# Powers on VectorE for chunk pairs, one contraction a chunk and a fixed instruction sequence in a gated mix of a diagonal state-space convolution and a gated linear unit

## The chip, the cores and the metric

The kernel runs on one core of a Trainium2 chip. The metric is the time of one execution on the device, in microseconds. The engines that matter are TensorE (PE in the profile, with its weight loads as PEld), VectorE (DVE), ScalarE (ACT), GpSimd (POOL), and SP, which issues nearly all DMAs.

## The reference, cut to what matters

All arrays are fp32: L = 2048 positions, D = 448 channels, N = 256 states, F = 1792 hidden units.

```python
dt = exp(log_dt)                                  # per channel
A  = -exp(log_A_real) + 1j * A_imag               # (D, N)
C  = (C_real + 1j * C_imag) * dt[:, None]
P  = exp((A * dt[:, None])[:, :, None] * arange(L))
K  = 2 * einsum("dn,dnl->dl", C, P).real          # the filter, (D, L)
y  = irfft(rfft(u.T, 2 * L) * rfft(K, 2 * L))[:, :L].T
a  = y + u * D_skip
b  = (sigmoid(u @ w_gate) * (u @ w_up)) @ w_down
g  = sigmoid((u * gate_w).sum(-1))
out = g * a + (1 - g) * b
```

## The kernel before, in words

Five kinds of work share the engines. (1) The gate `g`. (2) `params`: per half of the channels, amplitudes, phases and decay powers go through DRAM (`phd`, `bsd`). (3) `kgen`, the filter stage: 28 chunks of 16 channels make the filter `K`. (4) `Chain`: the convolution by an FFT written as matmuls, for two halves, with transposes through DRAM (`shf`) or, for one chain, on VectorE. (5) the gated unit: `glu_up`, `glu_mm` and `glu_down`, fp32 products as three matmuls of split operands (`wh`, `wl`, `xs`, `hh`, `hl`, `vh`, `vl`).

A position is l = 32 b + r. The filter of one channel is contracted over the 256 states from two factors, one for each part of the position; each factor is an amplitude (powers of the decay) times a sine or a cosine. In one chunk (`kgen`), for each of the two halves of the states (`half_chunk`, the states on the partitions):

- `turns` makes the angles with a matmul (`tp`, L1128), rounds them to whole turns on ScalarE (L1138, L1139), takes the whole turns off with a second matmul (L1141), and ScalarE makes `Abs` and `Sin` (L1143, L1144); L1158 makes the cosine. Cosines lie in `ec`, sines in `fr`.
- `powers` makes a table `tb` of decay powers, by GpSimd, one table for each chunk: (128, 32, 28), that is 16 channels of each of two halves of the states, and 28 powers of each, next to each other. Its instructions are L1105 to L1118.
- `outer` (L1165) multiplies two sets of those powers into the 96 amplitudes of each channel, in `es`: one VectorE product of 1024 elements (8 x 8 for 16 channels) and one of 512 (4 x 8).
- L1179 and L1181 (512 elements each) and L1183 and L1185 (1024 each) multiply amplitudes with cosines and sines, in `ec` and `es`.
- `g` contracts the half chunk (L1191): two sets of 16 products on quarters of the array's columns, into `kp`. After the second half ScalarE copies `kp` into `ke` (L1215), with a step of 56 elements in what it writes.

After 14 chunks a half of the filter goes to DRAM (`kd`) and its chain starts. The gated unit's matmuls fill TensorE between all this.

The order of the instructions on each engine is made before the kernel runs. `Plan.op` records each operation with what it reads and writes; `Plan.order` plays the program through a model of the engines (`Clock`) and emits, at each step, the ready operation with the lowest rank, where `RANK` gives ranks to groups of operations by engine, tile and priority. The engines then run these sequences in order, each waiting on semaphores.

Of the kernel before, what the change touches and what calls it, by code (L numbers as in the profile page):

```python
# [20 lines left out]
HD = 224  # L21
# [3 lines left out]
LADV = 0  # L25
CHANGE = 0.0


RANK = {
    ('Act', 'aci', 10): (671, -492),  # L30
    ('Act', 'aci', 19): (-256.5, 733.5),
    ('Act', 'acr', 10): (800, 106.5, -694.5),
    ('Act', 'acr', 19): (339, 607, -637),
    ('Act', 'ai', 10): 814,
    ('Act', 'ai', 19): -138,
    ('Act', 'bsx0', 10): (209.5, 93),
    ('Act', 'bsx0', 19): (192.5, 209),
    ('Act', 'ci', 10): (895.5, -362.5, 445.5),
    ('Act', 'ci', 19): (-615.5, 239, -615.5),
    ('Act', 'cr', 10): 118.5,  # L40
    ('Act', 'cr', 19): 618,
    ('Act', 'dots', 1): -520.5,
    ('Act', 'dots', 2): 579.5,
    ('Act', 'dots', 16): (-700, 879.5),
# [14 lines left out]
    ('Act', 'junk', 10): (143, 528),  # L59
    ('Act', 'junk', 19): (-337, -331.5, -344),  # L60
# [28 lines left out]
    ('DVE', 'aci', 10): 103,  # L89
    ('DVE', 'aci', 19): -245.5,  # L90
    ('DVE', 'acr', 10): 424.5,
    ('DVE', 'acr', 19): 900,
    ('DVE', 'ai', 10): -291.5,
    ('DVE', 'ai', 19): 529.5,
    ('DVE', 'bsx0', 10): (-548, 25),
    ('DVE', 'bsx0', 19): (-490.5, 740.5),
    ('DVE', 'ci', 10): 214.5,
    ('DVE', 'ci', 19): -661.5,
    ('DVE', 'cr', 10): (-364.5, 16.5),
    ('DVE', 'cr', 19): (93, -700),  # L100
    ('DVE', 'dt2', 10): -119,
    ('DVE', 'dtp', 10): 809.5,
    ('DVE', 'dtv', 10): 562.5,
    ('DVE', 'ec', 20): (492, 737, -509, -522.5, -148, -508.5, -540.5, -401.5),
    ('DVE', 'es', 20): (-560.5, -700, -613.5, -700, -577.5, -249, -611.5, -666.5),
    ('DVE', 'f', 10): (-484.5, -600.5),
    ('DVE', 'fx', 41): (-696.5, -696.5, -667, -700, 254, 114.5, -225.5, 268),
    ('DVE', 'gs', 1): 257.5,
    ('DVE', 'gs', 2): -362,
    ('DVE', 'gs', 16): (804, 891.5),  # L110
    ('DVE', 'gt', 1): (503.5, 457, 457, 457),
    ('DVE', 'gt', 2): (-418.5, -378, -416, -419),
    ('DVE', 'gt', 16): (-250.5, 93.5, -505.5, -522, -583.5, -600, -260, 548),
    ('DVE', 'half_pi', 0): 423.5,
# [20 lines left out]
    ('DVE', 'ones', 10): -432,  # L135
# [6 lines left out]
    ('DVE', 'skip', 20): 361,  # L142
# [5 lines left out]
    ('DVE', 'uax', 40): (733.5, -443, -259, 207, 252.5, -43, 547, -200.5),  # L148
# [1294 lines left out]
```

## Time and profile before

| | us |
|---|---|
| median of 3 runs (lowest to highest) | 742.1 (741.53 to 743.33) |
| the profiled execution's own time | 740.59 |
| its span, first to last instruction | 738.8 |
| granted clock of TensorE, mean | 0.979 |
| busy: PE, DVE, ACT, POOL | 688.4, 637.9, 523.7, 232.7 |

A row that groups instructions has the line, the engine and the operation, what it writes and reads, its shape and its count, then the time busy, the mean of one in ns, and the engine's idle time just before them with what ended it. A row of one line gives shortest, median and longest duration in ns and the first and the last start. A row of the chain of waits or of the timeline has its start and its length in us; on the chain a length ends where the next piece takes over. A row of stretches has the stretch, its length, each engine's busy time with its number of instructions, the granted clock, the DMA engines' share and GB/s.

### The profile page before, as it was taken

What the parts mean: (1) busy time and instruction counts of PE and PEld (TensorE: products, weight loads), DVE (VectorE), ACT (ScalarE), POOL (GpSimd) and SP (SyncE); (2) the same over time, 40 slices, a digit from 0 to 9 for tenths busy, and PEclk for the clock granted to TensorE, in tenths of its full rate; (3) what the DMA queues carried; (4) which work ended last, traced back from release to release, by engine and by line L of the source; (5) the groups of instructions that cost most, each with busy time, mean ns of one, the idle gap of its engine ahead of it and who ended that gap; (6) DMA issues with size and microseconds to landing.
All of it is one profiled execution on the core that took longest, in us unless ns stands there. A gap on an engine that the chain in (4) does not pass through costs nothing.

```text
span 738.8 us, 16536 instructions
## 1 busy us (share of the span) xinstructions
PE 688.4 (93%) x6628; PEld 498.6 (67%) x6628; DVE 637.9 (86%) x847; ACT 523.7 (71%) x962; POOL 232.7 (32%) x282
## 2 busy tenths in 40 slices
PE   4999899999999999978998899999999899999996
PEld 3788777677757776745666677777778566445863
DVE  6999998999999979999898779999995259775976
ACT  5578749999899779998998789999882342233110
POOL 0043446563455435434543324654400000000000
PEclk9999999999999999988999899999999999999998
DMA  9658337925949945469797913239516963787975
GB/s 291 200 122 217 108 79 203 239 91 171 202 121 223 219 107 160 171 175 204 183 232 180 220 45 125 86 133 175 119 40 131 271 226 100 249 304 207 168 191 142
DMA packets 98660, 126.12 MB, mean 171 GB/s; under 512 B 31224, under 2 KB 81080, under 8 KB 97560
## 3 DMA queue, kind: packets, MB, share of 16 engines
q1 hardware_dynamic: 98328, 124.61, 65.0%
q8 instruction: 52, 0.85, 0.5%
q0 software_dynamic: 256, 0.46, 0.3%
q14 instruction: 24, 0.20, 0.1%
HBM read 81.46 MB, written 43.58 MB: 169 GB/s over the span
## 4 chain that ended last, share of the span: by engine, by line
PE 42%; DVE 19%; ACT 16%; DMA 14%; issue 5%; SPq 3%; POOL 2%; ACTq 0%; DVEq 0%
PE kp_egp L1191 4%; PE gu_gps L1296 4%; PE dn_gps L1313 4%; PE gu_gps L1297 4%; PE gu_gps L1298 4%; PE dn_gps L1314 3%; PE dn_gps L1315 3%; DMA fx_fu<-shf 3%; SPq L615 3%; DVE es_eg L1165 2%; PE tp_egp L1128 2%; PE tp_egp L1141 2%; ACT nn_eg L1139 2%; DMA us<-fx_fu 2%; PE fps_fups L716 2%
## 5 line engine op out<-in xcount | busy, mean ns | idle before, releaser
L1296 PE MATMUL gu_gps<-xs_glu,wh_glu 128*128 128x512 f32 x336 | 138.1, 411 | 16.5 <-ACT wh_glu L1270 10.1
L1298 PE MATMUL gu_gps<-xs_glu,wl_glu 128*128 128x512 f32 x336 | 133.2, 397 | 0.4 <-DVE wl_glu L1272 0.4
L1297 PE MATMUL gu_gps<-xs_glu,wh_glu 128*128 128x512 f32 x336 | 133.3, 397 | 0.0
L1165 DVE TENSOR_TENSOR es_eg<-tb_eg 128x1024 f32<-128x1024 f32 x112 | 107.4, 988 | 7.0 <-POOL tb_eg L1115 3.7
L1313 PE MATMUL dn_gps<-vh_glu,hh_glu 128*128 128x448 f32 x224 | 87.9, 393 | 2.8 <-DVE ob_glu L1329 2.6
L1296 PEld LDWEIGHTS gu_gps<-xs_glu,wh_glu 128*128 128x128 f32 x336 | 64.1, 191 | 39.2 <-ACT wh_glu L1270 10.1
L1115 POOL TENSOR_TENSOR tb_eg<-tb_eg 128x96 f32<-128x96 f32 (+2 forms) x84 | 82.2, 982 | 6.2
L1314 PE MATMUL dn_gps<-vh_glu,hl_glu 128*128 128x448 f32 x224 | 82.6, 369 | 0.6 <-issue 0.4
L1315 PE MATMUL dn_gps<-vl_glu,hh_glu 128*128 128x448 f32 x224 | 82.3, 368 | 0.0
L1139 ACT ACTIVATE nn_eg<-fr_eg 128x512 fp32r<-128x512 f32 x112 | 75.0, 669 | 10.3 <-PE tp_egp L1141 10.1
L1329 DVE SCALAR_TENSOR_TENSOR ob_glu<-dn_gps,og,ob_glu 128x448 f32<-128x448 f32 x72 | 48.7, 677 | 30.2 <-PE dn_gps L1315 30.0
L1298 PEld LDWEIGHTS gu_gps<-xs_glu,wl_glu 128*128 128x128 f32 x336 | 64.0, 191 | 15.6 <-DVE wl_glu L1272 1.1
L1297 PEld LDWEIGHTS gu_gps<-xs_glu,wh_glu 128*128 128x128 f32 x336 | 64.2, 191 | 11.4
L1105 POOL MEMSET tb_eg<- 128x96 f32 x28 | 7.8, 283 | 201.1 <-DVE es_eg L1165 200.9
L1144 ACT ACTIVATE fr_eg<-tp_egp 128x512 f32<-128x512 f32 x112 | 69.9, 629 | 0.3 <-PE tp_egp L1141 0.3
L1185 DVE TENSOR_TENSOR es_eg<-fr_eg,es_eg 128x1024 f32<-128x1024 f32 x56 | 69.8, 1246 | 0.1
L1143 ACT ACTIVATE ec_eg<-tp_egp 128x512 f32<-128x512 f32 x112 | 69.4, 625 | 0.3 <-PE tp_egp L1141 0.2
L1183 DVE TENSOR_TENSOR ec_eg<-ec_eg,es_eg 128x1024 f32<-128x1024 f32 x56 | 69.5, 1241 | 0.1
L1138 ACT ACTIVATE fr_eg<-tp_egp 128x512 f32<-128x512 f32 x112 | 64.0, 636 | 7.2 <-DVE es_eg L1185 5.1
L1158 ACT ACTIVATE ec_eg<-ec_eg,half_pi 128x1024 f32<-128x1024 f32 x56 | 67.1, 1197 | 0.1
L1118 POOL TENSOR_TENSOR tb_eg<-tb_eg,bs_eg 128x32 f32<-128x32 f32 x84 | 62.0, 741 | 6.2
L1284 ACT ACTIVATE sg_glu<-gu_gps 128x512 f32<-128x512 f32 x56 | 34.0, 608 | 37.5 <-PE gu_gps L1301 35.3
(154 smaller groups left out, 1423.0 us busy)
## 6 DMA issues: line engine op xcount, KB each, us to landing
shf<-fx_fu SPq DMA_DIRECT2D x16, 896.0 KB, 4.1
fx_fu<-shf SPq DMA_DIRECT2D x16, 896.0 KB, 15.9
us<-fx_fu SPq DMA_DIRECT2D x16, 896.0 KB, 6.7
xr_glu<-in_w_dram SPq DMA_DIRECT2D x52, 256.0 KB, 3.0
ua_fk<-us SPq DMA_DIRECT2D x16, 448.0 KB, 6.0
uax_fk<-us SPq DMA_DIRECT2D x16, 448.0 KB, 4.5
vr_glu<-in_w_dram SPq DMA_DIRECT2D x28, 224.0 KB, 5.1
gt_pre<-in_u_dram SPq DMA_DIRECT2D x8, 448.0 KB, 4.9
```

Of the source, the lines that this page charges most:

```text
L1115: pool(96 * m, lambda n=n, m=m: G.tensor_mul(g3(n + 1, m), g3(1, m), g3(n, 1).to_broadcast([128, 32, 3, m])))
L1139: op("Act", c_act(512), lambda: S.activation(nn.real, fi(), AF.Copy, scale=-1.0, bias=MAGIC), [(fr, i)], [nn], prio)
L1144: op("Act", c_act(512, True), lambda: S.activation(fr[:, ds], tv(), AF.Sin, scale=TWO_PI), [tp], [(fr, i)], prio, table="sin")
L1165: V.tensor_mul(o.rearrange("p d (i k) -> p d i k", k=ny), x.unsqueeze(3).to_broadcast([128, 16, nx, ny]), y.unsqueeze(2).to_broadcast([128 ...
L1183: op("DVE", c_dve(1024), lambda: V.tensor_mul(ec[:, :, 32:96], ec[:, :, 32:96], es[:, :, 32:96]), [(es, 1), (es, 2)], [(ec, "p")], prio)
L1185: op("DVE", c_dve(1024), lambda: V.tensor_mul(es[:, :, 32:96], fr.real, es[:, :, 32:96]), [fr], [(es, 1), (es, 2)], prio)
L1296: T.matmul(p.real, wh[:, k, cs], x[:, k], start=(k == 0), stop=False)
L1297: T.matmul(p.real, wh[:, k, cs], x[:, 4 + k], start=False, stop=False)
L1298: T.matmul(p.real, wl[:, k, cs], x[:, k], start=False, stop=False)
L1313: T.matmul(p[:, :D], hh[:, ts], vh.real, start=(i == 0), stop=False)
L1314: T.matmul(p[:, :D], hl[:, ts], vh.real, start=False, stop=False)
L1315: T.matmul(p[:, :D], hh[:, ts], vl.real, start=False, stop=(i == len(fs) - 1))
```

## The change

- `powers` runs on VectorE, once for a pair of chunks. Its table is (128, 29, 64): 29 powers, and for each the 64 columns (two halves of the states by 32 channels) next to each other. There is one table instead of two; the decay powers' place in `bsd` is reordered for it. `outer` reads the table with channels and powers swapped in the access pattern.
- Cosines and sines lie in one tile `cs` (128, 2, 16, 96), three of them; the two products of 1024 elements are one of 2048, with the amplitudes read twice. `es` has one buffer.
- `contract` does both half chunks in one block, after the second.
- The four steps of a gated unit's matmuls wait for the halves of the activations and weights that they read, not for all.
- `vr` shares the raw tiles `xr` (4 now; 5 and one `vr` before); `sg` has 2 buffers for 3, `bs` 1 for 2; the phases are loaded for each chunk.
- The identity and the positions are loaded by SP and rounded by ScalarE; before, GpSimd's queue loaded them.
- `PLACE` gives every operation its place in its engine's sequence, in the stead of ranks; the model only merges the sequences, with issue times for each DMA.

```diff
-WB, ECB, FRB, TPB, KPB, GUB, FPS, SGB, XRB = 3, 2, 2, 2, 1, 2, 2, 3, 5
+WB, CSB, PHB, BSB, TPB, KPB, GUB, FPS, SGB, XRB = 3, 3, 2, 1, 2, 1, 2, 2, 2, 4
...
-        for key, x in RANK.items():
-            x = x if isinstance(x, tuple) else (x,)
-            for j, o in enumerate(kinds[key]):
-                o["prio"] = x[j * len(x) // len(kinds[key])]
+        for key, places in PLACE.items():
+            for o, place in zip(kinds[key], places, strict=True):
+                o["place"] = place
...
-    def powers(c, bs, prio):
-        tb = eg.tile("tb", TBB, (128, 32, 28))
+    def powers(bs, prio):
+        tb = state.get("tb")
+        if tb is None:
+            tb = state["tb"] = eg.tile("tb", 1, (128, 29, 64))
+            op("DVE", c_fast(192), lambda: V.memset(tb[:, 0:24].rearrange("p (g e) x -> p g e x", e=8)[:, :, 0], 1.0),
+               [], [(tb, 0)], prio)
         def g3(lo, n):
-            return tb[:, :, 0:24].rearrange("p d (g e) -> p d g e", e=8)[:, :, :, lo:lo + n]
+            return tb[:, 0:24].rearrange("p (g e) x -> p g e x", e=8)[:, :, lo:lo + n]
...
+        mul(256, lambda: V.tensor_copy(tb[:, 1:26:8], bs[:, 0:4]), c_fast)
         for n in (1, 2, 4):
             m = min(n, 3)
-            pool(96 * m, lambda n=n, m=m: G.tensor_mul(g3(n + 1, m), g3(1, m), g3(n, 1).to_broadcast([128, 32, 3, m])))
+            mul(192 * m, lambda n=n, m=m: V.tensor_mul(g3(n + 1, m), g3(1, m), g3(n, 1).to_broadcast([128, 3, m, 64])))
+        for e in range(25, 28):
+            mul(64, lambda e=e: V.tensor_mul(tb[:, e + 1], tb[:, e], bs[:, 4]))
...
         def r(k):
-            tt = tb[:, q0:q0 + 16]
+            tt = tb[:, :, q0:q0 + 16].rearrange("p e d -> p d e")
             if k == 0:
                 outer(es[:, :, 0:64], tt[:, :, 8:16], tt[:, :, 0:8])
...
-        op("DVE", c_dve(1024), lambda: V.tensor_mul(ec[:, :, 32:96], ec[:, :, 32:96], es[:, :, 32:96]),
-           [(es, 1), (es, 2)], [(ec, "p")], prio)
-        op("DVE", c_dve(1024), lambda: V.tensor_mul(es[:, :, 32:96], fr.real, es[:, :, 32:96]),
-           [fr], [(es, 1), (es, 2)], prio)
+        op("DVE", c_dve(2048), lambda: V.tensor_mul(
+            cs[:, :, :, 32:96], cs[:, :, :, 32:96], es[:, :, 32:96].unsqueeze(1).to_broadcast([128, 2, 16, 64])),
+           [(es, 1), (es, 2)], cos + sin, prio)
+        return cs
+
+    def contract(parts, kp, prio):
         def g():
-            for e in (ec, es):
-                for q in range(4):
-                    for j in range(4):
-                        T.matmul(kp[32 * j:32 * j + 32, q], e[:, 4 * j + q, 64:96], e[:, 4 * j + q, 0:64], ...)
-        op("PE", c_mm4(64, 32, QUARTERS), g, [ec, es], [kp], prio)
+            for cs in parts:
+                for z in range(2):
+                    for q in range(4):
+                        for j in range(4):
+                            T.matmul(kp[32 * j:32 * j + 32, q], cs[:, z, 4 * j + q, 64:96], cs[:, z, 4 * j + q, 0:64], ...)
+        op("PE", c_mm4(64, 64, QUARTERS), g, parts, [kp], prio)
...
-            op("PE", c_mm(512, 3 if k < 3 else 2), lambda k=k: g(k), [x, wh, wl], [p], pe)
+            z = 2 * (k // 2)
+            op("PE", c_mm(512, 3 if k < 3 else 2), lambda k=k: g(k), [(x, (0, z)), (x, (1, z)), (wh, z), (wl, z)], [p], pe)
```

More of the change, by code (lines that the diff above doesn't have):

```diff
@@ new lines @@
+PLACE = {
+    ('Act', 'aci', 10): (19, 46,),
+    ('Act', 'aci', 19): (73, 100,),
+    ('Act', 'acr', 10): (15, 44, 57,),
+    ('Act', 'acr', 19): (78, 97, 109,),
[26 rows of a table added]
+    ('Act', 'dots', 1): (39,),
+    ('Act', 'dots', 2): (53,),
+    ('Act', 'dots', 16): (71, 87,),
[18 rows of a table added]
+    ('Act', 'idn', 10): (20,),
+    ('Act', 'junk', 10): (42, 77,),
+    ('Act', 'junk', 19): (89, 96, 122,),
[12 rows of a table added]
+    ('Act', 'pos_sb', 10): (32, 98,),
[24 rows of a table added]
+    ('DVE', 'aci', 10): (56,),
+    ('DVE', 'aci', 19): (127,),
+    ('DVE', 'acr', 10): (91,),
+    ('DVE', 'acr', 19): (167,),
[17 rows of a table added]
+    ('DVE', 'dtp', 10): (46,),
+    ('DVE', 'dtv', 10): (33,),
[14 rows of a table added]
+    ('DVE', 'half_pi', 0): (2,),
[22 rows of a table added]
+    ('DVE', 'ones', 10): (0,),
[7 rows of a table added]
+    ('DVE', 'skip', 20): (30,),
[11 rows of a table added]
+    ('DVE', 'uax', 40): (734, 738, 744, 745, 755, 754, 763, 764, 768, 767, 774, 773, 777, 778, 785, 784, 811, 812,
[131 rows of a table added]
@@ L243 @@
 HB = 3
-PEM = (1, 1)
 GLO = 0
@@ L367, in run @@
         if o["size"]:
-            self.free[e] = t + (self.ISSUE if e == "SP" else self.CAST)
+            self.free[e] = t + (o["issue"] if e == "SP" else self.CAST)
             self.wire = max(self.wire, self.free[e] + 1000.0) + o["cost"]
@@ L474, in order @@
         clock = Clock(engines)
-        cand = {e: [o for o in ops if o["eng"] == e and need[o["i"]] == 0] for e in engines}
+        queue = {e: sorted((o for o in ops if o["eng"] == e), key=lambda o: -o["place"]) for e in engines}
         users, done, left, end, slots = {}, {}, {}, {}, {}
@@ L485, in start_of @@
         def start_of(o):
+            if need[o["i"]]:
+                return None
             t, n = ready[o["i"]], {}
@@ L502, in order @@
             for e in engines:
-                lo, ok = None, []
-                for o in cand[e]:
-                    t = start_of(o)
-                    if t is not None:
-                        ok.append((t, o))
-                        lo = t if lo is None else min(lo, t)
-                if lo is None:
-                    continue
-                te = clock.when(e, lo)
-                if best is None or te < best[0]:
-                    best = (te, e, ok)
+                t = start_of(queue[e][-1]) if queue[e] else None
+                if t is not None:
+                    te = clock.when(e, t)
+                    if best is None or te < best[0]:
+                        best = (te, e)
             if best is None:
                 raise RuntimeError("no instruction can start")
-            te, e, ok = best
-            def rank(o):
-                change = e == "PE" and clock.mode is not None and o["cost"][0][0] != clock.mode
-                return o["prio"] + (CHANGE if change else 0.0), o["i"]
-            o = min((o for t, o in ok if t <= te), key=rank)
-            cand[e].remove(o)
+            te, e = best
+            o = queue[e].pop()
             fin = clock.run(o, te)
@@ L543, in order @@
                 need[d] -= 1
-                if need[d] == 0:
-                    cand[p["eng"]].append(p)
             seq.append((te, len(seq), o))
@@ L698, in stage1 @@
                     dma(lambda ls=ls, z=z: x[64 * z:64 * z + 64, ls], lambda ls=ls: ap()[:, ls], 64 * 4 * HD * 4, src,
-                        [(x, (z, r)) for r in range(4 * q, 4 * q + 4)], prio, HALF)
+                        [(x, (z, r)) for r in range(4 * q, 4 * q + 4)], prio, HALF, 700.0)
             for q in range(4):
@@ L877, in gated_mix @@
     P = 112
-    steps, POW = (64.0, 1.0, 512.0, 8.0), (2, 0, 3, 1)
+    steps, POW = (64.0, 1.0, 512.0, 8.0), (2, 0, 4, 1)
     class Params:
@@ L1113, in powers @@
         for n in (1, 2, 4):
             m = min(n, 3)
-            pool(96 * m, lambda n=n, m=m: G.tensor_mul(g3(n + 1, m), g3(1, m), g3(n, 1).to_broadcast([128, 32, 3, m])))
-        pool(32, lambda: G.tensor_scalar(t(24), b(4), 1.0, 0.0, op0=ALU.mult, op1=ALU.add), c_pool1)
-        for e in range(24, 27):
-            pool(32, lambda e=e: G.tensor_mul(t(e + 1), t(e), b(3)))
+            mul(192 * m, lambda n=n, m=m: V.tensor_mul(g3(n + 1, m), g3(1, m), g3(n, 1).to_broadcast([128, 3, m, 64])))
@@ L1151, in half_chunk @@
+        op("Act", c_act(512, True), lambda: S.activation(cs[:, 1, ds, 32:96], block(tp), AF.Sin, scale=TWO_PI),
+           [tp], [(cs, ("s", i))], prio, table="sin")
+    def half_chunk(c, nh, ph, tb, prio):
+        cs = eg.tile("cs", CSB, (128, 2, 16, 96))
+        es = eg.tile("es", 1, (128, 16, 96))
         for i in range(2):
             tp = egp.tile("tp", TPB, (128, 512))
-            turns(c, nh, i, ph, fr, tp, ec, on_pe, prio)
-        if not on_pe:
-            op("Act", c_act(1024), lambda: S.activation(ec[:, :, 32:96], fr.real, AF.Abs), [fr], [ec], prio)
-            op("Act", c_act(1024), lambda: S.activation(fr.real, fr.real, AF.Sin, scale=-TWO_PI), [], [fr], prio,
-               table="sin")
+            turns(c, nh, i, ph, cs, tp, prio)
+        cos, sin = [(cs, ("c", i)) for i in range(2)], [(cs, ("s", i)) for i in range(2)]
@@ L1198, in kgen @@
         if c % 2 == 0:
-            ph = state["ph"] = eg.tile("ph", 2, (96, 2, N))
-            for i in range(2):
-                dma(lambda i=i: ph[:, i], lambda i=i: phd[:, 16 * (c + i):16 * (c + i) + 16], 96 * 1024,
-                    [(phd, (k, c // 14)) for k in range(6)], [(ph, i)], prio, 115.0)
-            bs = state["bs"] = eg.tile("bs", 2, (128, 5, 64))
+            bs = state["bs"] = eg.tile("bs", BSB, (128, 5, 64))
             dma(lambda: bs.real, lambda: bsd[:, c // 2].rearrange("p (a d) -> p a d", a=5), 128 * 1280,
                 [(bsd, (i, c // 14)) for i in range(5)], [bs], prio)
-        ph, tb = state["ph"], powers(c, state["bs"], prio)
+            powers(bs, prio)
+        tb, ph = state["tb"], eg.tile("ph", PHB, (96, N))
+        dma(lambda: ph.real, lambda: phd[:, 16 * c:16 * c + 16], 96 * 1024,
+            [(phd, (k, c // 14)) for k in range(6)], [ph], prio, 115.0, 700.0)
         if cc == 0:
@@ L1210, in kgen @@
         kp = egp.tile("kp", KPB, (128, 4, 64))
-        for nh in range(2):
-            half_chunk(c, nh, ph, tb, kp, prio)
+        contract([half_chunk(c, nh, ph, tb, prio) for nh in range(2)], kp, prio)
         def ev():
@@ L1263, in glu_w @@
             glu_split(wr, lambda wr=wr: wr.real, wh, wl, lambda t, k=k: t[:, k:k + 2], k, 512, prio, 7 * H + f // 2)
-        vr = glu.tile("vr", 1, (128, D))
-        dma(lambda: vr.real, lambda: w2[128 * f:128 * f + 128], 128 * D * 4, [], [vr], prio)
-        glu_split(vr, lambda: vr.real, vh, vl, lambda t: t.real, 0, D, prio, 7 * H + f // 2)
+        vr = raw_tile(H == 0 and f < 2)
+        vw = lambda: vr.v("p a b -> p (a b)")[:, :D]
+        dma(vw, lambda: w2[128 * f:128 * f + 128], 128 * D * 4, [], [vr], prio)
+        glu_split(vr, vw, vh, vl, lambda t: t.real, 0, D, prio, 7 * H + f // 2)
         ws[H, f] = (wh, wl, vh, vl)
@@ L1376, in gated_mix @@
     params(1, sizes, P_PRO1)
+    for i in range(2):
+        rounded(pos, post, 96, 512, 512 * i)
     kgen_consts(P_E)
```

152 lines of the change are left out of this document (40 added, 112 removed), and 438 rows, old and new, of tables (PLACE, RANK).

## The prediction

> **What bounds the kernel now.** I read the page's head first, then busy time by stage, then the groups by shape, and last the chain at both ends of the filter stage.
>
> ```profile
> span 738.8 us, 16536 instructions
> ## 1 busy us (share of the span) xinstructions
> PE 688.4 (93%) x6628; PEld 498.6 (67%) x6628; DVE 637.9 (86%) x847; ACT 523.7 (71%) x962; POOL 232.7 (32%) x282
> ```
>
> PE leads on the whole span, but the change acts in one stage. The filter stage runs from the first outer product at 123.7 us to the last VectorE multiply, started at 553.4 us:
>
> ```profile
> L1165 DVE TENSOR_TENSOR es_eg<-tb_eg x112: 673/1207/1855, 123.7 to 548.6; 128x1024 f32<-128x1024 f32 x56, 128x512 f32<-128x512 f32 x56
> ...
> L1185 DVE TENSOR_TENSOR es_eg<-fr_eg,es_eg x56: 1206/1214/1893, 132.5 to 553.4; 128x1024 f32<-128x1024 f32 x56
> ...
> L1179 DVE TENSOR_TENSOR ec_eg<-ec_eg,es_eg x56: 673/692/1398, 128.7 to 549.9; 128x512 f32<-128x512 f32 x56
> ```
>
> Busy time in the stretches before, in and after it:
>
> ```profile
> core 0: us, PE busy (x) PEld busy (x) DVE busy (x) ACT busy (x) POOL busy (x), PEclk, DMA share, GB/s
> 0.00:127.00 127.00, 110.75 (x487) 90.39 (x488) 114.22 (x213) 87.65 (x156) 44.14 (x48) 1.00 0.64 174
> 127.00:555.00 428.00, 405.46 (x5050) 295.82 (x5048) 402.87 (x480) 388.68 (x718) 188.60 (x234) 0.97 0.64 157
> 555.00:739.00 184.00, 172.19 (x1094) 112.40 (x1093) 120.86 (x157) 47.34 (x90) 0.00 (x0) 0.98 0.72 200
> ```
>
> In the filter stage PE, DVE and ACT are busy 405, 403 and 389 of 428 us: three engines within a few per cent of each other. VectorE has 25 us of room there. More VectorE work than that lengthens the stage; the 63 us that it is idle after 555 us are out of reach, since the tail needs the finished filter. So the prediction is a VectorE sum over this stage, plus what happens at its two ends.
>
> **Part 1, powers leave GpSimd.** VectorE's groups in the stage, by shape, and the longest wait of all:
>
> ```profile
> L1165 DVE TENSOR_TENSOR es_eg<-tb_eg 128x1024 f32<-128x1024 f32 x56 | 69.8, 1246 | 6.3 <-POOL tb_eg L1115 3.7 <-PE kp_egp L1191 1.3 <-POOL tb_eg L1108 0.5
> L1185 DVE TENSOR_TENSOR es_eg<-fr_eg,es_eg 128x1024 f32<-128x1024 f32 x56 | 69.8, 1246 | 0.1
> L1183 DVE TENSOR_TENSOR ec_eg<-ec_eg,es_eg 128x1024 f32<-128x1024 f32 x56 | 69.5, 1241 | 0.1
> L1179 DVE TENSOR_TENSOR ec_eg<-ec_eg,es_eg 128x512 f32<-128x512 f32 x56 | 45.0, 804 | 10.2 <-ACT ec_eg L1158 9.8
> L1181 DVE SCALAR_TENSOR_TENSOR es_eg<-fr_eg,es_eg 128x512 f32<-128x512 f32 x56 | 42.2, 754 | 0.5
> L1165 DVE TENSOR_TENSOR es_eg<-tb_eg 128x512 f32<-128x512 f32 x56 | 40.9, 730 | 0.6 <-POOL tb_eg L1118 0.6
> L1288 DVE TENSOR_TENSOR hl_glu<-sg_glu,hh_glu 128x512 fp32r<-128x512 f32 x56 | 39.5, 713 | 7.1 <-ACT hh_glu L1287 7.0
> L1272 DVE TENSOR_TENSOR wl_glu<-xr_glu,wh_glu 128x512 fp32r<-128x512 f32 x52 | 37.9, 749 | 0.0
> ...
> POOL tb_eg L1105 <- DVE es_eg L1165: 200.9, 26, 12.4
> ```
>
> GpSimd waited 201 us for a free table, so its powers were ahead of need except at the start; taking them away ends waits of only some 5 us (3.7, 0.6, 0.5). What VectorE gains is duration. The quickest 1024- and 512-wide operations took 1206 and 673 ns; the means lie above by 40, 40 and 35 ns on the wide ones and by 131, 81, 57, 40 and 76 ns on the narrow ones. Times 56 (52 for the last) that is 28 us; some of L1272 and L1288 lies outside the stage, so I credit 26, on the reading that GpSimd's arithmetic causes all of it. The bound from below is 0.
>
> What comes back as VectorE work, per chunk pair: a copy of 256 elements, products of 192, 384 and 576, three of 64. Durations overlap the next instruction, so steps in the chain price them better:
>
> ```profile
> 110.81 3.70 DMA bs_eg<-bsd
> ...
> 114.58 2.79 POOL tb_eg L1108 x2
> 117.37 4.12 POOL tb_eg L1115 x6
> 121.50 1.22 POOL tb_eg L1116 x2
> 122.71 2.93 POOL tb_eg L1118 x5
> ...
> 138.16 1.13 DVE ec_eg L1183
> ...
> 141.63 0.60 DVE ec_eg L1179
> 142.23 0.54 DVE vl_glu L1272
> 142.77 0.60 DVE es_eg L1181
> 143.37 1.74 DVE es_eg L1165 x2
> ```
>
> 1024 in 1.13 and 512 in 0.60 us give 1.035 ns an element and 0.07 us an instruction. The products: 0.27 + 0.47 + 0.67 + 3 x 0.14 = 1.83; the copy 0.2 to 0.33, taken 0.2. So 2.03 us a pair, 28 us for 14: the relief and the new work cancel.
>
> **Part 2, the layout of the table.** This edit is not in the name of the change. Before, the table is (32 channels, 28 powers), and the eight powers that the outer product's second operand runs through lie next to each other; its first operand holds one element for eight results. These reads go at full speed (1.74 for 1024 + 512, as 1.13 + 0.61). After, it is (29 powers, 64 channels): the second operand steps 64 elements, 256 bytes, at every result. The trace shows no such VectorE product. Its nearest rows are operations that step far at every element:
>
> ```profile
> L730 DVE STREAM_TRANSPOSE fx_fk<-fx_fk 128x896 f32<-128x896 f32 x16 | 31.1, 1966 | 1.7 <-ACT fx_fk L719 1.7
> L1215 ACT ACTIVATE ke_eg<-kp_egp 128x256 f32<-128x256 f32 x28 | 19.5, 696 | 4.3 <-PE kp_egp L1191 4.3
> L719 ACT ACTIVATE fx_fk<-fps_fkps 128x448 f32<-128x448 f32 x16 | 7.8, 543 | 16.8 <-PE fps_fkps L716 16.8
> ...
> 604.91 3.69 DVE L730 STREAM_TRANSPOSE fx_fk<-fx_fk 128x896 f32<-128x896 f32 x2 [1.66 <-ACT fx_fk L719]
> ```
>
> The transpose reads and writes with a step of 224 elements: two in 3.69 us, about 1.80 each, (1.80 - 0.07) / 896 = 1.93 ns an element, 0.89 above the plain rate. ScalarE's copy of 256 elements with a written step of 56 took 696 ns where 448 elements in long runs took 543: at least 0.60 ns an element dearer, on one stepping side. So the price for one stepping operand lies between 0 (if transposing itself is what costs) and 0.89 (if the read alone makes it); half of the transpose's excess is 0.45. I take 0.65, between that half and the whole, near ScalarE's one-sided 0.60. A half chunk has 1024 + 512 such elements: 1.0 us, times 56 = 56 us; bounds 0 and 77.
>
> The Trainium skill's page "Vector Engine (DVE) Microarchitecture Reference", section "Measured stream behaviour on trn2", says that a port keeps its full rate only over runs of at least two adjacent 4-byte words: 1.73 ns a column with one source jumping at every element against 1.054 contiguous, and 1.98 with all operands jumping. By that the edit costs an estimated 58 us; the transpose's 1.93 agrees with its 1.98, and no run here shows the one-source case. The same table has 2.50 for a step of 24 words, which would make it an estimated 125 us.
>
> **Part 3, sine and cosine in one tile.** Two 1024-wide products (1.13 each) become one of 2048: 2048 x 1.035 ns + 0.07 = 2.19, so -0.07 x 56 = -4 us.
>
> **Part 4, one contraction a chunk.** On PE, around one contraction of before:
>
> ```profile
> 200.02 0.39 PE L1297 MATMUL gu_gps<-xs_glu,wh_glu 128*128 128x512 f32 x1
> 200.25 0.39 PE L1298 MATMUL gu_gps<-xs_glu,wl_glu 128*128 128x512 f32 x1
> 200.57 0.65 PE L1191 MATMUL kp_egp<-ec_eg 128*32 128x64 f32 x32
> 201.04 0.63 PE L1191 MATMUL kp_egp<-es_eg 128*32 128x64 f32 x32
> 201.60 0.50 PE L1300 MATMUL gu_gps<-xs_glu,wh_glu 128*128 128x512 f32 x1
> 201.94 0.40 PE L1301 MATMUL gu_gps<-xs_glu,wl_glu 128*128 128x512 f32 x1
> ```
>
> Starts are 0.23 us apart in a run, 0.32 into the contraction and 0.34 after it: 0.2 us a change of form. 28 fewer save at least 5.6 us of PE. I count nothing: PE is no longer what ends the stage. If Part 2 costs nothing, this is what keeps PE (405 busy) clear of VectorE. The contraction now waits for both halves; behind it on PE stand the gated unit's matmuls, and ScalarE's half after next waits for the tile. With three tiles it can run one half ahead, which is 1.74 + 0.60 + 0.60 + 2.19 = 5.1 us of VectorE work and covers two blocks of 1.03 (200.57 to 201.60); nothing counted.
>
> **Part 5, gated unit by quarters; loads; one raw tile fewer.** Units may start on half the weights; PE's gain is hidden as in Part 4. The copies of identity and positions leave GpSimd's queue for three more issues on SP and three short ScalarE copies, in the first 127 us, where ScalarE is busy 88: hidden. Each chunk's phase load waits on SP for the chunk two before, and the raw weight loads behind it with it; with four shared raw tiles for six, 0, up to the 25 us of slack.
>
> **Part 6, the fixed sequence.** Counting it off: 32, 31, 32 and 35 of VectorE's sg, hl, wl and ob steps lie in the stage, against 29, 27, 28 and 32 in the trace: 14 more at 0.60, +8 us. The first contraction stands behind 113 steps on gu, of 135 before. The stage's start: from the landed amplitudes (110.81 + 3.70 = 114.5) GpSimd's tables let the first outer product begin at 123.7, 9.2 us later; VectorE needs 2.0: -7. Of the 8 us moved out from ahead of it some 3 come off as well, and of the 22 gu steps (2.75 matmuls of 0.23 us each, 14 us of PE) I add 2. Start 123.7 -> 112. In the tail PE, 172 of 184 us busy, has nearly the same steps: 184 kept.
>
> **Sum.** VectorE in the stage: 403 - 26 + 28 + 56 - 4 + 8 = 465 us; with 13 us of idle (half of now, as it is alone the bound) 478. 112 + 478 + 184 = 774 us of span. The profiled execution took 740.59 us for its 738.8, so +1.8: **775 us**, against that 740.59 (the median of the runs is 742.1). About 0.3%, 2.2 us, is what can be told from no change.
>
> **Rivals.** (a) *Steps are free*, and the 1.93 ns are the transpose's own. VectorE 409, idle 15: 112 + 424 + 184 = 720, **722 us**, faster. For it: a read repeated eight times already costs nothing. Against: ScalarE's row, which transposes nothing. (b) *The read alone costs the whole 0.89 or more*: 77 us, **797 us** and up; its lower edge is where the read takes more than the write. (c) *The order stalls though steps are free*: phase and weight loads behind one another on SP leave VectorE idle for twice today's 25 us instead of 15: 722 + 35 = **757 us**; for it only ScalarE's waits of 9.8 us ahead of L1179 stand, which show how little is spare.
>
> **How the numbers follow.** Forecast 0.62 (its own range 757 to 797), (a) 0.22, (b) 0.10, (c) 0.04, and 0.02 that gains and price cancel. Slower 0.76, same 0.02, faster 0.22. The range of 8 in 10 takes in most of (a) and the foot of (b): 716 to 805.
>
> **What would show it.** Right: the 1024-wide outer product near 1.9 us (1.25 now), the 512-wide near 1.05, the other 512-wide ones at 0.68, VectorE over 96% busy in the stage, PE below 90%, first outer product near 112 us. Wrong: outer products at 1.21 us; then (a) or (c), told apart by the stage's length. A tail far from 184 us would break the sum's last term.

## The result, and the profile after

| | before | after |
|---|---|---|
| median of the runs (lowest to highest) | 742.25 (741.53 to 743.33) | 779.48 (777.94 to 781.22) |
| after : before, 95% interval | | 1.0501 (1.0471 to 1.0531) |
| the profiled execution, its span | 740.59, 738.8 | 778.36, 776.6 |
| stage starts, first outer product | 123.7 | 118.0 |
| stage, first outer product to the end of the last VectorE product | 430.9 | 480.2 |
| from there to the end | 184.2 | 178.4 |

All in us. One of the four executions in experiment 2 (817.74 us) was in a slower state and is left out there. The change made the kernel 5% slower. The filter stage grew by 49.3 us; its start and the tail gave back 11.5.

The head of the page and its chain of work that ended last, after, and then the same line of the chain before:

```profile
span 776.6 us, 16302 instructions
## 1 busy us (share of the span) xinstructions
PE 695.5 (90%) x6628; PEld 502.4 (65%) x6628; DVE 705.8 (91%) x890; ACT 532.1 (69%) x965; POOL 29.3 (4%) x28
...
## 4 chain that ended last, share of the span: by engine, by line
DVE 49%; PE 33%; issue 10%; ACT 6%; DMA 2%; SPq 0%; DVEq 0%; ACTq 0%
```

```profile
PE 42%; DVE 19%; ACT 16%; DMA 14%; issue 5%; SPq 3%; POOL 2%; ACTq 0%; DVEq 0%
```

VectorE now has more busy time than PE, and half of the chain, where it had a fifth. Busy time by stretch, after, cut at the stage's own ends (columns as before):

```profile
core 0: us, PE busy (x) PEld busy (x) DVE busy (x) ACT busy (x) POOL busy (x), PEclk, DMA share, GB/s
0.00:118.00 118.00, 101.49 (x430) 81.28 (x431) 104.84 (x211) 83.35 (x149) 29.33 (x28) 0.99 0.63 164
118.00:598.00 480.00, 421.97 (x5098) 307.58 (x5097) 477.60 (x521) 401.01 (x726) 0.00 (x0) 0.96 0.57 144
598.00:776.00 178.00, 172.00 (x1101) 113.50 (x1101) 123.32 (x160) 47.77 (x91) 0.00 (x0) 1.00 0.78 212
```

In the stage VectorE is busy 477.6 of 480 us, 99.5%, and PE 422, 88%. VectorE alone sets its length. What it does there, its groups by shape, after:

```profile
L1242 DVE TENSOR_TENSOR cs_eg<-cs_eg,es_eg 128x2048 f32<-128x2048 f32 x56 | 128.2, 2289 | 0.6
L1223 DVE TENSOR_TENSOR es_eg<-tb_eg 128x1024 f32<-128x1024 f32 x56 | 117.7, 2101 | 0.4
L1223 DVE TENSOR_TENSOR es_eg<-tb_eg 128x512 f32<-128x512 f32 x56 | 61.7, 1102 | 0.0
...
L1239 DVE SCALAR_TENSOR_TENSOR cs_eg<-cs_eg,es_eg 128x512 f32<-128x512 f32 x56 | 38.4, 687 | 0.0
L1237 DVE TENSOR_TENSOR cs_eg<-cs_eg,es_eg 128x512 f32<-128x512 f32 x56 | 38.4, 686 | 0.1
```

The outer products went from 1246 and 730 ns to 2101 and 1102. The two 512-wide products with cosines and sines went the other way, from 804 and 754 to 686 and 687, with GpSimd quiet. One group of PE says who waits now, the gated unit's `dn` matmuls, after and then before:

```profile
L1376 PE MATMUL dn_gps<-vh_glu,hh_glu 128*128 128x448 f32 x224 | 89.8, 401 | 26.0 <-DVE ob_glu L1392 20.7
```

```profile
L1313 PE MATMUL dn_gps<-vh_glu,hh_glu 128*128 128x448 f32 x224 | 87.9, 393 | 2.8 <-DVE ob_glu L1329 2.6
```

PE stood 20.7 us for VectorE's step that reads that PSUM tile. Before, the whole idle time of this group was 2.8 us. And the start of the stage, in the chain of waits, after (start, length):

```profile
106.28 0.20 DVE tb_eg L1182
...
109.13 0.14 DVE tb_eg L1185
...
111.51 0.47 DVE tb_eg L1185
111.97 0.54 DVE th_pro L975
112.51 0.67 DVE tb_eg L1185
113.18 0.54 DVE th_pro L978
113.72 0.59 DVE ob_glu L1392
...
116.85 0.13 DVE tb_eg L1187
...
118.12 2.09 DVE es_eg L1223 x2
```

The powers are made from 106 us on, between steps of the parameters (`pro`) and of the gated unit on the same engine. The chain passes through VectorE's own queue and no longer through a landed load: the load of the decay powers (`bs`) is issued at 96.1 us now, at 110.8 before.

### The profile page after: what moved, and what is told of

The parts are those of the page before. It is cut to its first block, busy times and chain, and to the rows that moved or that the text cites. A ratio compares the mean times of both kernels' runs of the same rounds, so it can differ in the third digit from the quotient of the medians.

```text
span 776.6 us, 16302 instructions
## 1 busy us (share of the span) xinstructions
PE 695.5 (90%) x6628; PEld 502.4 (65%) x6628; DVE 705.8 (91%) x890; ACT 532.1 (69%) x965; POOL 29.3 (4%) x28
## 4 chain that ended last, share of the span: by engine, by line
DVE 49%; PE 33%; issue 10%; ACT 6%; DMA 2%; SPq 0%; DVEq 0%; ACTq 0%
DVE es_eg L1223 13%; DVE cs_eg L1242 11%; PE gu_gps L1358 4%; DVE cs_eg L1239 4%; DVE cs_eg L1237 4%; PE gu_gps L1359 4%; PE gu_gps L1360 4%; PE dn_gps L1376 3%; PE dn_gps L1377 3%; DVE ob_glu L1392 3%; PE dn_gps L1378 3%; DVE tb_eg L1185 3%; DVE wl_glu L1334 2%; DVE sg_glu L1347 2%; DVE hl_glu L1350 2%
## 5 line engine op out<-in xcount | busy, mean ns | idle before, releaser
L1223 DVE TENSOR_TENSOR es_eg<-tb_eg 128x1024 f32<-128x1024 f32 x112 | 175.7, 1602 | 0.4
L1358 PE MATMUL gu_gps<-xs_glu,wh_glu 128*128 128x512 f32 x336 | 139.6, 416 | 20.7 <-DVE sg_glu L1347 9.7
L1359 PE MATMUL gu_gps<-xs_glu,wh_glu 128*128 128x512 f32 x336 | 135.4, 403 | 0.0
L1242 DVE TENSOR_TENSOR cs_eg<-cs_eg,es_eg 128x2048 f32<-128x2048 f32 x56 | 128.2, 2289 | 0.6
L1376 PE MATMUL dn_gps<-vh_glu,hh_glu 128*128 128x448 f32 x224 | 89.8, 401 | 26.0 <-DVE ob_glu L1392 20.7
L1198 ACT ACTIVATE cs_eg<-tp_egp 128x512 f32<-128x512 f32 x112 | 67.2, 604 | 20.0 <-PE tp_egp L1194 18.8
L1376 PEld LDWEIGHTS dn_gps<-vh_glu,hh_glu 128*128 128x128 f32 x224 | 43.0, 192 | 54.8 <-DVE ob_glu L1392 32.9
L1200 ACT ACTIVATE nn_eg<-cs_eg 128x512 fp32r<-128x512 f32 x112 | 71.3, 637 | 9.6 <-PE tp_egp L1203 8.4
L1205 ACT ACTIVATE cs_eg<-tp_egp 128x512 f32<-128x512 f32 x112 | 66.0, 602 | 12.8 <-PE tp_egp L1203 12.5
L1206 ACT ACTIVATE cs_eg<-tp_egp 128x512 f32<-128x512 f32 x112 | 67.3, 604 | 8.1 <-PE tp_egp L1203 7.9
L1359 PEld LDWEIGHTS gu_gps<-xs_glu,wh_glu 128*128 128x128 f32 x336 | 65.3, 194 | 11.5
L1254 PE MATMUL kp_egp<-cs_eg 128*32 128x64 f32 x3584 | 59.6, 223 | 7.5 <-DVE cs_eg L1242 6.2
L1254 PEld LDWEIGHTS kp_egp<-cs_eg 128*32 128x32 f32 x3584 | 53.3, 112 | 19.3 <-issue 9.4
L1216 ACT ACTIVATE cs_eg<-cs_eg,half_pi 128x1024 f32<-128x1024 f32 x56 | 65.2, 1164 | 0.3
L1203 PE MATMUL tp_egp<-nn_eg,idn 128*128 128x512 f32 x112 | 49.9, 446 | 8.5 <-ACT nn_eg L1200 6.8
```

The lines of the kernel that those rows point to most:

```text
L1200: op("Act", c_act(512), lambda: S.activation(block(nn), cs[:, 1, ds, 32:96], AF.Copy, scale=-1.0, bias=MAGIC), [(cs, ("s", i))], [nn], prio)
L1206: op("Act", c_act(512, True), lambda: S.activation(cs[:, 1, ds, 32:96], block(tp), AF.Sin, scale=TWO_PI), [tp], [(cs, ("s", i))], prio, ta ...
L1223: V.tensor_mul(o.rearrange("p d (i k) -> p d i k", k=ny), x.unsqueeze(3).to_broadcast([128, 16, nx, ny]), y.unsqueeze(2).to_broadcast([128 ...
L1242: op("DVE", c_dve(2048), lambda: V.tensor_mul(cs[:, :, :, 32:96], cs[:, :, :, 32:96], es[:, :, 32:96].unsqueeze(1).to_broadcast([128, 2, 1 ...
L1254: T.matmul(kp[32 * j:32 * j + 32, q], cs[:, z, 4 * j + q, 64:96], cs[:, z, 4 * j + q, 0:64], start=cs is parts[0] and z == 0 and q == 0, s ...
L1358: T.matmul(p.real, wh[:, k, cs], x[:, k], start=(k == 0), stop=False)
```

## The experiments

The theory: the outer product's running operand steps 64 elements at every result, that alone makes VectorE the bound, and everything else nearly cancels. The rivals: the powers themselves, the order of the sequence, the contraction, or GpSimd's relief that does not come.

"Stage" below is the same stretch as in the table, read from each kernel's trace, and "busy" the busy time in it.

**1. The table with powers next to each other.** Only the table's layout of the change is turned; everything else stays.

```diff
-            tb = state["tb"] = eg.tile("tb", 1, (128, 29, 64))
+            tb = state["tb"] = eg.tile("tb", 1, (128, 64, 29))
...
-            tt = tb[:, :, q0:q0 + 16].rearrange("p e d -> p d e")
+            tt = tb[:, q0:q0 + 16]
```

> The changed kernel with one thing undone: the table of powers is (64 channels, 29 powers), so that the powers lie next to each other and the outer product's running operand no longer steps. Sequence, tiles, contraction and waits stay as changed. Theory (the step costs the time): the 1024-wide outer product falls from 2.10 to 1.21 us and the 512-wide from 1.10 to 0.68, which is (0.89 + 0.42) x 56 = 73 us of VectorE work; the powers themselves now step in part (some 1600 elements a pair, up to 1.4 us x 14 = 19 us back). The filter stage goes from 480 to 425-435 us and the span to 720-735. Rival (the fixed sequence, the single contraction or the later waits cost it): the outer products get shorter but the stage stays near 480 with idle time on VectorE, time 765 or more.

Measured: 730.33 us (726.32 to 732.38), 0.9793 of before (0.9736 to 0.9851). A second set of runs, beside those of experiment 5:

> The changed kernel with the near layout of the powers' table once more, as the measure for the three kernels beside it: 726-735 us, ratio to the kernel before 0.975-0.985.

Measured: 730.02 us (728.25 to 736.25), 0.9848 (0.9810 to 0.9885). Page, stretch of the stage and groups by shape, of this second run:

```profile
PE 681.2 (93%) x6628; PEld 497.1 (68%) x6628; DVE 642.5 (88%) x890; ACT 528.1 (72%) x965; POOL 29.8 (4%) x28
...
PE 62%; ACT 14%; DVE 13%; DMA 6%; issue 4%; SPq 1%; ACTq 0%; DVEq 0%
```

```profile
119.00:550.00 431.00, 406.17 (x5046) 300.87 (x5048) 413.67 (x522) 397.15 (x726) 0.00 (x0) 0.98 0.65 160
```

```profile
L1223 DVE TENSOR_TENSOR es_eg<-tb_eg 128x1024 f32<-128x1024 f32 x56 | 68.3, 1220 | 0.4
...
L1223 DVE TENSOR_TENSOR es_eg<-tb_eg 128x512 f32<-128x512 f32 x56 | 38.4, 685 | 0.0
```

The outer products are back at 1220 and 685 ns, the chain is PE's again (62%; VectorE 13%), and the stage takes 430.7 us, 49.5 less than after the change. So the layout alone carries more than the whole loss: without it the change is a gain of 1.5 to 2% over before. The stage itself is not shorter than before (430.7, and 434.6 in the profile of the first set, against 430.9). The gain lies at the two ends: the stage starts at 119.1 and the tail is 179.7, together 9.1 us less. The near layout has a price of its own, on the powers: they take 37.2 us of VectorE in all, counted from start to start, against 29.6 in the stepping layout.

**2. The step without the rest of the change.** The kernel before, with only its GpSimd table turned; the running operand steps 32 elements here.

```diff
-        tb = eg.tile("tb", TBB, (128, 32, 28))
+        tb = eg.tile("tb", TBB, (128, 28, 32))
...
-            tt = tb[:, q0:q0 + 16]
+            tt = tb.v("p e x -> p x e")[:, q0:q0 + 16]
```

> The kernel before with this one part of the change alone: its table (still by GpSimd, one for each chunk) is laid out (28 powers, 32 channels), so that the running operand steps 32 elements. Theory (the step costs the time): outer products near 2.1 and 1.1 us, 60 to 74 us more VectorE work in a stage that had 25 us idle, time 780-800. Rival (the layout is harmless): outer products at 1.25 and 0.73, time 742-748.

Measured: 804.47 us (803.93 to 806.62), 1.0815 (1.0757 to 1.0872). Page and groups by shape:

```profile
PE 713.3 (89%) x6628; PEld 503.5 (63%) x6628; DVE 711.5 (89%) x847; ACT 527.4 (66%) x962; POOL 345.7 (43%) x282
```

```profile
L1166 DVE TENSOR_TENSOR es_eg<-tb_eg 128x1024 f32<-128x1024 f32 x56 | 118.8, 2122 | 3.6 <-POOL tb_eg L1119 1.4 <-PE kp_egp L1192 1.3 <-POOL tb_eg L1116 0.9
...
L1166 DVE TENSOR_TENSOR es_eg<-tb_eg 128x512 f32<-128x512 f32 x56 | 63.2, 1129 | 1.6 <-POOL tb_eg L1119 1.6
```

The step costs the same in the other kernel (2122 and 1129 ns), so it belongs to the operand and not to the sequence around it. The time came out above what was expected: in the stage, now 491.1 us, VectorE's busy time rose by 73 us (405 to 478), and of its 25.8 us of idle only 12.7 took that up. GpSimd's busy time rose too, from 232.7 to 345.7 us, and little of that is its own stepping. Its products among the powers, before (shortest, median and longest in ns):

```profile
L1115 POOL TENSOR_TENSOR tb_eg<-tb_eg x84: 363/1120/3056, 117.3 to 524.0; 128x96 f32<-128x96 f32 x28, 128x192 f32<-128x192 f32 x28, 128x288 f32<-128x288 f32 x28
...
L1118 POOL TENSOR_TENSOR tb_eg<-tb_eg,bs_eg x84: 269/603/1313, 122.6 to 527.7; 128x32 f32<-128x32 f32 x84
```

The same two here:

```profile
L1116 POOL TENSOR_TENSOR tb_eg<-tb_eg x84: 348/1212/10425, 117.9 to 580.4; 128x96 f32<-128x96 f32 x28, 128x192 f32<-128x192 f32 x28, 128x288 f32<-128x288 f32 x28
...
L1119 POOL TENSOR_TENSOR tb_eg<-tb_eg,bs_eg x84: 245/584/12336, 123.7 to 585.8; 128x32 f32<-128x32 f32 x84
```

The shortest are no longer than before and the medians hardly; it is the longest that grew, to 10.4 and 12.3 us, also in the second row, whose 32 elements lie next to each other in the turned table. By their spans GpSimd's powers ran beside VectorE's outer products for 99 us in all, 44 before. This fits a wait for VectorE; no run takes it apart.

**3. The price by the step.** The change, with the outer product's operands replaced by views that step differently from chunk to chunk; each line of the profile is one pair of steps (held operand, running operand), in elements. The filter's values are others.

```diff
-                outer(es[:, :, 0:64], tt[:, :, 8:16], tt[:, :, 0:8])
+                stepped(es[:, :, 0:64], 8, 8)
...
+STEPS = [(1, 1), (1, 2), (1, 4), (1, 8), (1, 16), (1, 24), (1, 32), (1, 64), (64, 1), (64, 64), (1, 128), (1, 12)]
```

> The changed kernel, in which the two operands of the outer product are read at other places of the table with other steps, a different pair of steps in each of twelve classes of chunks; the powers' values that the filter gets are therefore others (that part of the computation is changed), all instruction counts and sizes are the same. Only the durations by line are read. Theory (a running operand that leaves its neighbours costs, a held one does not): held 1 and running 1 takes 1.21 us for 1024, running 64 alone 2.0-2.1, held 64 alone 1.21-1.3, both 64 2.10; the price starts between steps 2 and 4 and is the same from 8 on. By the table of the Trainium skill's page Vector Engine (DVE) Microarchitecture Reference, section Measured stream behaviour on trn2, step 24 would take an estimated 2.6 us and the large steps an estimated 1.8. Rival (the held operand's step costs as well): held 64 alone at 1.5 or more.

Measured, groups by shape. In order of lines: (1,1), (1,2), (1,4), (1,8), (1,16), (1,24), (1,64), (64,1), (64,64):

```profile
L1241 DVE TENSOR_TENSOR es_eg<-tb_eg 128x1024 f32<-128x1024 f32 x6 | 7.3, 1213 | 0.0
...
L1243 DVE TENSOR_TENSOR es_eg<-tb_eg 128x1024 f32<-128x1024 f32 x6 | 7.3, 1222 | 0.1
...
L1245 DVE TENSOR_TENSOR es_eg<-tb_eg 128x1024 f32<-128x1024 f32 x6 | 12.1, 2023 | 0.0
...
L1247 DVE TENSOR_TENSOR es_eg<-tb_eg 128x1024 f32<-128x1024 f32 x6 | 12.9, 2150 | 0.0
...
L1249 DVE TENSOR_TENSOR es_eg<-tb_eg 128x1024 f32<-128x1024 f32 x4 | 7.9, 1963 | 0.0
...
L1251 DVE TENSOR_TENSOR es_eg<-tb_eg 128x1024 f32<-128x1024 f32 x4 | 10.8, 2708 | 0.0
...
L1255 DVE TENSOR_TENSOR es_eg<-tb_eg 128x1024 f32<-128x1024 f32 x4 | 8.2, 2038 | 0.1
...
L1257 DVE TENSOR_TENSOR es_eg<-tb_eg 128x1024 f32<-128x1024 f32 x4 | 4.8, 1211 | 0.0
...
L1259 DVE TENSOR_TENSOR es_eg<-tb_eg 128x1024 f32<-128x1024 f32 x4 | 8.4, 2101 | 0.0
```

Steps of 1 and 2 are free; from 4 on the price is there at once and hardly grows: 1963 to 2150 ns, and 2708 at 24. The three pairs not shown, with running steps of 12, 32 and 128, took 2018, 2053 and 2000 ns. The operand that is held for eight results may step 64 elements for nothing (1211). So it is the running operand alone, and hardly the distance: of the steps tried, only 2 would have saved the table after.

**4. GpSimd's relief by itself.** The kernel before with tables made for the first two chunks only and read by all (the powers of 26 chunks are left out). First with the sequence made anew:

```diff
-        ph, tb = state["ph"], powers(c, state["bs"], prio)
+        if c < 2:
+            state["tb", c] = powers(c, state["bs"], prio)
+        ph, tb = state["ph"], state["tb", c % 2]
```

> The kernel before, with GpSimd making the powers of the first two chunks only and all later chunks reading these two tables: the powers of the other 26 chunks are left out. Theory (GpSimd's arithmetic stretches VectorE's): the 512-wide products of the stage go from 804, 754 and 730 ns to 680-700, the wide ones from 1246 to 1210-1220, 20 to 27 us less VectorE time in the stage; since TensorE is as busy there, the time falls by less, to 720-738. Rival (the stretching has another cause): durations as before, time 735-742 from the 5 us of waits alone.

Measured: 769.35 us, one run. The durations fell as expected, yet the time rose. With fewer operations the ranks give other sequences, so a second kernel kept every engine's sequence of before and only issued no GpSimd powers after the first two chunks:

> As the run with two tables (GpSimd makes the powers of the first two chunks only, the other 26 chunks' powers are left out), but every other instruction stands in the order of the kernel before: the order is planned with GpSimd's steps in it and they are then not emitted. Theory (that run was slow because the planner made another order, not because GpSimd was quiet): durations of VectorE's products as there, 680-690 and 1215-1220 ns, VectorE some 25 us less busy in the stage, and now a time below the kernel before: 722-738. Rival (GpSimd's absence itself brings the loss): 755 or more, with the tail again above 200 us.

Measured: 740.82 us (735.59 to 743.09), 0.9961 (0.9937 to 0.9985), less of a gain than expected. Groups by shape:

```profile
L1169 DVE TENSOR_TENSOR es_eg<-tb_eg 128x1024 f32<-128x1024 f32 x56 | 68.4, 1221 | 13.8 <-PE kp_egp L1195 13.5
...
L1183 DVE TENSOR_TENSOR ec_eg<-ec_eg,es_eg 128x512 f32<-128x512 f32 x56 | 38.5, 687 | 16.7 <-ACT ec_eg L1162 16.5
```

In the stage VectorE's busy time fell from 405 to 384 us, 21 of the 26 expected, and the time by hardly 3. What was saved turned into waits: 13.5 us for PE ahead of the outer product (1.3 before) and 16.5 for ScalarE ahead of the 512-wide product (9.8 before). Three engines bind this stage, and relief of one is worth little while the other two stand at 407 and 391. The 28.5 us between the two kernels come with the other sequence, of which there is one execution only. Their granted clock, in tenths over 40 slices of the span, remade sequence first:

```profile
PEclk9999999999999989999999999999999999999666
```

```profile
PEclk9999999999999999988999899999999999999998
```

In the remade one the last three slices, which are tail, ran at 0.6; its tail took 204.4 us and that of the kept one 184.8, which is 19.6 of the 28.5 us. PE was busy for 170 us of the one and 174 of the other, so it also stood idle for longer. Whether the sequence or that one execution made the clock dip no run settles.

**5. The other parts of the change, taken out of the version with the near table.** The contraction in two blocks again, the first 4.5 places ahead of the second:

```diff
-            for cs in parts:
-                for z in range(2):
+            for z in range(2):
...
-        contract([half_chunk(c, nh, ph, tb, prio) for nh in range(2)], kp, prio)
+        for nh in range(2):
+            contract(half_chunk(c, nh, ph, tb, prio), nh, kp, prio)
```

> The near layout, and the contraction again one block for each half chunk: the first half's block stands four TensorE steps ahead of the second's, a place that the sequence allows; all else as in the kernel beside it. Theory (TensorE is not what ends the filter stage, VectorE and the order are): 28 changes of form more, 5.6 us of TensorE work, but at most 3 us more time. Rival (TensorE ends the stage once the step's price is gone): 5 us or more above the kernel beside it.

Measured: 749.85 us (747.39 to 754.24), 1.0112 (1.0074 to 1.0149), some 20 us above the near table's 730. The expectation missed. The stage took 447.4 us, 16.7 more. PE's busy time in it rose by 5.5 us (405.8 to 411.3), close to the 5.6 of the changes of form, though the granted clock there was 1.00 against 0.98, so the two do not compare exactly; the rest goes with a wait that came to 0.4 us in the near table's run. Waits (us in total, times, longest):

```profile
PEld kp_egp L1252 <- ACT ke_eg L1275: 18.2, 14, 3.1
```

There is one `kp` tile, and the earlier first block needs it before ScalarE has copied the last chunk out. How two blocks would do with two such tiles was not run, so the 14 us apart from the form may be this placement's and not the block's.

Waits on whole tiles in the gated unit:

```diff
-[(x, (0, z)), (x, (1, z)), (wh, z), (wl, z)], [p], pe)
+[x, wh, wl], [p], pe)
```

> The near layout, and the gated unit's matmuls waiting again for the whole activations and weights. Theory (the waits by quarters move only the first matmul, by some 1.5 us, and TensorE's start is not on the chain): within 2 us of the kernel with the near layout. Rival (they keep TensorE fed in the stage): 5 us or more above it.

Measured: 729.01 us (728.02 to 732.00), 0.9828 (0.9799 to 0.9858): no difference to the near table's 0.9848. PE's first matmul of the gated unit began at 8.66 us here, 8.59 after the change and 10.08 before, so the finer waits are not what lets it begin earlier.

The sequence by the ranks and the model of before, instead of fixed places:

```diff
+RANK = { ... }
...
-        for key, places in PLACE.items():
-            for o, place in zip(kinds[key], places, strict=True):
-                o["place"] = place
+        for key, x in RANK.items():
+            x = x if isinstance(x, tuple) else (x,)
+            for j, o in enumerate(kinds[key]):
+                o["prio"] = x[j * len(x) // len(kinds[key])]
```

> The near layout, and the order made again by the planner of the kernel before with its ranks (new operations have the ranks of their stage). Theory (the fixed sequence carries the gain that the near layout shows over the kernel before): 742 us or more, with the loss in the stage and in the tail. Rival (the gain comes from the powers and the contraction): within 5 us of the kernel with the near layout.

Measured: 775.43 us (773.38 to 782.12), 1.0468 (1.0425 to 1.0511). The stage took 438.2 us, the tail 209.7. The ranks were made for other operations, so these 45 us are an upper bound of what fixed places are worth; that the sequence alone can move this kernel by nearly as much as the layout does is shown. The mean granted clock was 0.952 in the profiled execution, 0.987 with the near table; what part of the 45 us that makes is not shown.

The last three products of a pair back on GpSimd:

```diff
-            mul(64, lambda e=e: V.tensor_mul(tb[:, :, e + 1], tb[:, :, e], bs[:, 4]))
+            op("Pool", c_pool(64), lambda e=e: G.tensor_mul(tb[:, :, e + 1], tb[:, :, e], bs[:, 4]), [bs], [(tb, 1)], prio)
```

> The near layout, with the last three products of each pair (64 elements each) on GpSimd instead of VectorE, which loses 8.6 us of instructions; GpSimd works 42 short products, and the 512-wide outer product of the pair's first half chunk waits for the last. Theory (VectorE still sets the length of the stage): 3 to 8 us below the kernel with the near layout, 722-727. Rival (three engines share the bound, and the new wait for GpSimd eats the gain): 728-735.

Measured: 730.37 us (727.38 to 733.39), 0.9831 (0.9797 to 0.9864): no gain, as the rival had it, though VectorE's busy time in the stage fell from 413 to 410. Group by shape:

```profile
L1184 POOL TENSOR_TENSOR tb_eg<-tb_eg,bs_eg 128x64 f32<-128x64 f32 x42 | 45.4, 1080 | 366.4 <-DVE tb_eg L1179 332.4 <-DMA fx_fu<-shf 31.8
```

One takes 1080 ns there on average (358 at the shortest), against 280 on VectorE in the same layout (experiment 1). The simplest version that beats both kernels is thus the change with the near table, 730 us.

## Why the prediction was right, point by point

The forecast, that stepping makes VectorE the bound of the stage and the kernel slower, held: 775 was said, 779.5 measured, against a profiled execution of 778.4. (The last step of the sum, 774 and 1.8, makes 776.) The signs named ahead came out: 2101 and 1102 ns (1.9 and 1.05 us were said), 687 for the other 512-wide ones, 99.5% for VectorE, 88% for PE. One did not: the first outer product at 118, not near 112. The sum by its terms, in us:

| term | predicted | measured | from |
|---|---|---|---|
| VectorE in the stage before | 403 | 405.1 | cut at the stage's own ends |
| GpSimd's relief | -26 | -21.2 | experiment 4, same sequence |
| powers on VectorE | +28 | +27.6 | trace after, in the stage |
| the step | +56 | +72.3 | outer products from start to start, after against near table |
| merged product | -4 | -6.5 | `cs` products after against `ec` and `es` products in experiment 4 |
| gated-unit steps in the stage | +8 | +0.5 | after against experiment 4 |
| VectorE's sum | 465 | 478 | |
| idle | +13 | +2.4 | |
| stage | 478 | 480.2 | |
| start | 112 | 118.0 | |
| tail | 184 | 178.4 | |

- **The step** was mis-sized: 0.65 ns an element was taken, from between ScalarE's 0.60 and the transpose's 0.89. The durations give (2101 - 1219) / 1024 = 0.86 and (1102 - 684) / 512 = 0.82. A read alone costs nearly what the transpose's read and write cost together, so the transpose's excess should not have been shared out between its two sides. The step's 72 us are nearer to rival (b)'s 77 than to the forecast's 56: with them the forecast's own sum would have given 792 us. Rival (a), free steps at 722 us, falls with experiment 3; had steps been free, the near table's 730 shows about what would have come.
- **The relief** was real and GpSimd's, 21 of 26. Rival (a) counted it in full where steps are free; in the kernel before, where they are free, it was worth hardly 3 us (experiment 4). In the changed kernel it counts because VectorE is alone the bound.
- **The step's worth** is likewise not its 72 us. With the near table VectorE has 17 us of idle in the stage and 7 us more on powers, and the stage is 49.5 us longer with the step than without.
- **The gated unit's steps** were miscounted: places were counted from the first table operation, not from the first outer product. The trace after has 31, 30, 30 and 32 of sg, hl, wl and ob in the stage, 29, 28, 28 and 32 before: 6 more and not 14, with 2 vl fewer. All gated-unit work together is 87.0 us there, against 86.5 in experiment 4, since each of the four kinds takes 0.60 us on average and not 0.62.
- **Idle** fell to 2.4: with one engine short, there is always something ready for it. "Half of now" was too much.
- **The start** failed as a step: it was priced as the landing of the decay powers (in the prediction's words, the amplitudes) plus 2 us of products, with gated-unit steps taken off. The chain shows what sets it: the load lands early enough, and VectorE's own queue decides, in which the powers stand between parameter and gated-unit steps from 106 to 117 us.
- **The tail** came 5.8 us shorter, for which there was no term. It is as short with the near table (179.7), with whole waits (179.6) and with GpSimd's last products (179.9), and 209.7 with the other sequence; that the fixed places make it is argued by this and not shown part by part. The granted clock has a share as well: 0.98 before and 1.00 after in the tail's rows, an estimated 3 to 4 of the 5.8 us if PE bound the whole tail.
- **Contraction, waits, loads** at nothing: for the waits shown (experiment 5); the loads were not tried by themselves. For the contraction the form is worth 5.5 us of PE, as worked out, and the one PSUM tile was not thought of.

So the direction and the cause were right, and the time came out this close by luck, because errors cancelled: the step (16 us), the relief (5) and the start (6) were set too low, the unit's steps (7.5), the idle (11) and the tail (6) too high.

## What to carry to other kernels

When work moves to another engine, look first at what the move does to the layout that the widest reader sees; here the layout, and not the moved work, decided, and the operand that runs fastest must have its elements next to each other (a step of 2 was still free here, one of 4 was not). Where three engines are busy 90 to 95% of a stage, taking work off one is worth a small part of itself, while adding to one is paid in full once the idle time that it can use is gone (12.7 of 25.8 us in experiment 2). A trial that changes the number of operations in a planned sequence must keep the sequence, or it measures the planner as well.

## What the runs showed of the hardware that was not expected

- The price of a stepping read is a threshold and not a slope: 1222 ns for 1024 elements at a step of 2, 2023 at 4, 2038 at 64, with 2708 at 24 as an exception. An operand whose element is held for eight results pays nothing for its step (1211). The Trainium skill's page "Vector Engine (DVE) Microarchitecture Reference", section "Measured stream behaviour on trn2", has full rate only for runs of two or more adjacent words. The trace differs: a step of 2 words is free here. The page has 1.73 ns a column for one source that jumps 4 KiB at every element, against 1.054, which is 0.68 more; at 64 words (256 bytes) the trace's excess is (2038 - 1213) / 1024 = 0.81 ns. For a step of 24 words the page has 2.50, with both sources or the destination stepping, 1.45 more than its plain rate; here one stepping read is (2708 - 1213) / 1024 = 1.46 ns above the plain one.
- GpSimd's products of 32 elements took up to 12.3 us in the kernel whose outer products step (experiment 2), where the shortest of them took 0.25; before, the longest took 1.3.
- GpSimd's arithmetic beside VectorE lengthened VectorE's 512-wide products from 684 to 687 ns to 730 to 804, and the 1024-wide ones from about 1220 to 1246 (experiment 4, where all but the first two chunks' powers are left out, against the kernel before).
